# Another order of steps in an attention-and-ReGLU kernel

## The chip, the core and the metric

The kernel runs on one core of a Trainium2 chip. The core has a matmul engine (TensorE, in the profile PE, its weight loads PEld), a vector engine (VectorE, DVE), an engine for activations (ScalarE, ACT), a general one (GpSimd, POOL) and SyncE (SP), which here only issues transfers. Each takes its instructions in the order in which the program has them. The metric is the device time of one launch in microseconds.

## The reference

```python
B, N, m, C = (4, 12416, 32, 128)
def mab(q, kv):
    s = scale * (q @ kv.transpose(0, 2, 1))
    s = s - s.max(-1, keepdims=True)
    a = np.exp(s)
    a /= a.sum(-1, keepdims=True) + 1e-09
    return a @ kv
h = mab(I, x)
attn = mab(x, h)
...
gate = np.maximum(x @ w_gate, 0.0)
val = x @ w_val
out = gate * val @ w_out
```

For each of four batches, 32 inducing vectors attend to the 12,416 rows of x and give h (32 x 128). Then every row attends to those 32 vectors; the result goes through a feed-forward layer with 1,536 hidden units, where "x" is the attention's result.

## The kernel before

A row's attention output is a weighted mean of 32 vectors. The sign of a gate is settled for each hidden unit and batch; with it the layer's output is a quadratic form in the 32 softmax weights. The kernel works on that form: products of two weights are exponentials of sums of two scores, and a table T per batch (built from h and the three weight matrices) takes 512 such products and 128 single terms to the 128 outputs. Were a sign not certain, a general kernel would run at the end; the flag for this is read near the end by all engines.

A batch has 97 tiles of 128 rows. Four tiles make a block, four blocks a quad "q", six quads and one rest tile a batch. These are the steps, and where their instructions run:

- **E** (`scores`, L558): two matmuls of 32 rows by 512 columns, each on its own row group of PE, make sums of scores in `e_ps` (two buffers); ACT takes the exponential of both into an `F` tile (L576; 20 buffers). 49 per batch.
- **O** (`outputs`, L583): one tile of 128 rows of the result. Four matmuls L591 with F as weights and one L593 with the single terms `p`, 128 rows by 129 columns. After three tiles DVE divides (`rzo` L607, `osb` L608) out of `o_ps` (two buffers); after six, SP stores `osb` (four buffers, L617). 97 per batch.
- **p** (lane of `plan_phase1`, L673): the first attention of the next batch: for batch 1 six turns on PE (L698), then for all `score` (L707, ACT L709), `sums` (L720, L729, DVE L742), `h_end1`, `h_end2` (the DVE chain in `halves`, L130), four `gates` (PE L347, ACT L362, DVE L364), signs and `masked` (L451).
- **u** (products and tables): DVE makes products of gate and value columns (L473, L482), PE sums them with `wo` into the tables (L519, ACT's cast L522; the fifth table L539, DVE L546). T has two buffers, by batch.
- **s**: scores of a quad for the second attention (`pair_out`, L648: PE L372, DVE L628 and L640), and the bounds for the certainty of the signs (L381 to L446, two DVE reductions, one matmul, three POOL instructions).
- **x** (`pair_exp`, L652): ACT's exponential of a quad's scores (L655), which O reads as `p`.
- **l** (`load`): POOL starts the load of one quad of x (`load_x`, L82), cast to 16 bits. Where a turn has been issued since the last load, POOL first reads one value of the turned tile (L681), so that the load starts after it has landed. `x16` has nine buffers.
- **t** (`turn`): SP starts a transposing transfer of the last loaded quad (`turn_x`, L88, the instruction at L91). `xT` has twelve buffers. SP's queue is the one that the stores use.

A first part (`first_batch`, L158) and the first steps of batch 0 stand in a fixed order. From there the string `ORDER` says which step comes next: each letter takes the next step of its lane. Each lane keeps its own order; the string sets how the lanes are interleaved, and with that the order on every engine. The loop at the end of `quadratic_body`:

```python
for step in ORDER:
    if step == "E":
        scores(*next(units))
    elif step == "O":
        b, t = next(tiles)
        g = b * NSLOT + t // TPB
        outputs(b, t)
        if g == B * NSLOT - 3 and t % TPB == 0:
            cond = nc.values_load(flag.left[0:1, 0:1])
    else:
        lanes[step].pop(0)()
```

Below, E71 or O128 is the state after so many E's and O's of the string.

Of the kernel before, what the change touches and what calls it, by code (L numbers as in the profile page):

```python
# [26 lines left out]
def quadratic_body(ctx, tc, x, inducing, moe_w_gate, moe_w_val, moe_w_out, out):  # L27
# [860 lines left out]


ORDER = (  # L890
    "EOpOsExOpOEEpOOOEOOEppOEuEpOOOpEEspOOxOOpOllEElsplOOpOEEOlOOOppEEpOppOpEsEpOpOOEEpOOpEpE"
    "OOOxOsEEOOOpOpEOOpOpOtEpEOpOOEOOpOtEOEtOEuOuOOuxtOOEtusEOuOuEOOOEuuOOxEsuuEuOOOEslsOEOuu"
    "OsuluEEOpOOOEEuOEpEuOpOEEuuuOOxuOOuEEssOOOxOEEpOpuOOOtEuuEupOOtpOEEOuOOOEEOppOOOEEsOOOOl"
    "OlxEEOOpxOOOEEOlOOlOpOEEspxOOOOEEOlOOOpOEEOOOpEOEppOOEEOOpOtpEEpOOpOOOOEEOOtpOOpOEOEOOpO"
    "EsExOOOtutOEEuOOOutOEOuussEOEOOOExuuuOOEElsOOOupluuOEsEsOOEOuxOuEEpuOpEuEuOuOxOOEEOuOOOu"
    "uEOOEsuEuOOEEtuOOpEOuOupOEuEOOtOpEsEOOpuEEsOOOOOEEOOOxOpsEEOOOOpOOEEpOpOOOxOEEspOOpOEOpE"
    "OEppEOOEOOppOEOppOOEpEOOOpOOEOOEpOxOOuOEEuOOOsEOuOOuusEOEOuEOOuEEuuOOOEOOOEsuEOxuOOOEEus"
    "sOOuExuOOOxuEEsuEOuOEOOuEOOEOOOxEuEuOuOOOOEsEuOuOEEOOOOOuEEuuOOOOOEEOuOsEEOOOEOOOxOOOEEO"
    "OOOOOEEOOxOOOOEEOOOOOOEEOOOOOxOEEOOOOOOEEsOOxOOOEEOOOOOsEEOOOOOsEEOOOOsOOEEOOOOOOEEOsOOE"
    "OEOOOxsOOEEOOOOOEsOEOOOxOEEOOOOOOOOOOOO"  # L900
)


# [202 lines left out]
```

## Time and profile before

| | |
|---|---|
| median of 4 runs | 273.33 us (272.33 to 274.58) |
| the profiled execution | 272.81 us |
| its span, first to last instruction | 270.9 us |
| PE, ACT, DVE, POOL busy | 252.2, 228.3, 214.5, 27.3 us |
| start of the first step of the string | about 38.3 us |
| end of the last O's matmuls | 264.4 us |
| transfers | 48.38 MB, mean 179 GB/s |

Busy time is the sum of an engine's instructions; PE's are modelled as to their ends. In a timeline, x4 stands for four instructions of one line that follow each other; the time in brackets is the engine's idle time before the first of them, and what ended it. Loads of one quad land after 10.3 us at the median, turns after 5.0 us, stores after 3.0 us.

### The profile page before, as it was taken

To read this page: it belongs to the slowest core of one execution; us is meant where nothing else is said; L and a number is where in the kernel's file an instruction comes from. 1 tells how busy PE (TensorE), PEld (TensorE's weight loads), DVE (VectorE), ACT (ScalarE), POOL (GpSimd) and SP (SyncE) were. 2 spreads that over 40 slices of the span, in tenths; PEclk is the share of its full clock that TensorE was granted. 3 is DMA by queue.
4 is the path that set the end of the run, shared out by engine and by line. 5 is a ranking of instruction groups with operands and counts; after the bars stand their busy time and mean duration, and the time that the engine had idled before them with its cause. 6 is when DMAs were issued, how large, how long until landed. Compare 5 with 4: busy or idle time off the path is not lost.

```text
span 270.9 us, 9520 instructions
## 1 busy us (share of the span) xinstructions
PE 252.2 (93%) x4029; PEld 188.1 (69%) x4029; DVE 214.5 (79%) x583; ACT 228.3 (84%) x305; POOL 27.3 (10%) x71
## 2 busy tenths in 40 slices
PE   2997799999999999999999999999899999999990
PEld 0795678777676777776667777777677778878770
DVE  4565969757999997775999998778999997688661
ACT  4134699999998999999799999999899989988940
POOL 8372000120000200400003000000010000000000
PEclk9999799999999999999999999999999999999997
DMA  7999986999899989899998979332331234344333
GB/s 184 203 209 204 213 171 79 272 212 246 180 227 189 204 247 210 203 248 261 213 222 214 220 205 186 119 117 85 152 120 60 116 123 154 155 167 161 134 145 110
DMA packets 48738, 48.38 MB, mean 179 GB/s; under 512 B 35472, under 2 KB 36656, under 8 KB 48688
## 3 DMA queue, kind: packets, MB, share of 16 engines
q1 hardware_dynamic: 41520, 33.74, 43.9%
q0 software_dynamic: 6880, 13.50, 27.9%
q8 instruction: 33, 0.54, 0.8%
q10 hardware_dynamic: 288, 0.46, 0.5%
q14 instruction: 17, 0.14, 0.2%
HBM read 27.80 MB, written 25.43 MB: 196 GB/s over the span
## 4 chain that ended last, share of the span: by engine, by line
PE 79%; DVE 8%; ACT 8%; issue 3%; POOL 0%; ACTq 0%; DVEq 0%; POOLq 0%
PE o_ps L591 32%; PE e_ps L569 16%; PE o_ps L593 7%; ACT F L576 5%; PE T_ps L519 3%; PE s_ps L707 3%; PE T_ps L505 3%; PE s_ps L372 3%; DVE osb L608 2%; PE hz_ps L729 2%; PE xT_ps L262 2%; PE T_ps L539 1%; PE s_ps L273 1%; PE hz_ps L720 1%; PE xT_ps L698 1%
## 5 line engine op out<-in xcount | busy, mean ns | idle before, releaser
L576 ACT ACTIVATE F<-e_ps 128x1024 f16<-128x1024 f32 x192 | 185.6, 1026 | 14.6 <-PE e_ps L569 12.1
L591 PE MATMUL o_ps<-T,F 128*128 128x129 f16 x1536 | 129.4, 221 | 1.8 <-DVE osb L608 1.0
L591 PEld LDWEIGHTS <-F 128*128 128x128 f16 x1536 | 98.6, 97 | 27.9 <-issue 19.5
L593 PE MATMUL o_ps<-T,p 128*128 128x129 f16 x388 | 84.5, 218 | 0.0
L608 DVE TENSOR_TENSOR osb<-o_ps,rzo 128x384 f32<-128x384 f32 x132 | 72.5, 549 | 4.8 <-DVE rzo L607 0.2
L569 PE MATMUL e_ps<-sc,sel 32*128 32x512 f16 x384 | 59.6, 382 | 0.5 <-ACT F L576 0.3
L593 PEld LDWEIGHTS <-p 128*128 128x128 f16 x388 | 37.9, 98 | 0.4
L607 DVE RECIPROCAL rzo<-o_ps 128x3 f32<-128x3 f32 x132 | 23.1, 175 | 18.6 <-PE o_ps L593 17.3
L569 PEld LDWEIGHTS <-sel 32*128 32x128 f16 x384 | 16.2, 91 | 18.2 <-issue 5.4
L628 DVE TENSOR_SCALAR sc<-s_ps 128x512 f16<-128x512 f32 (+1 forms) x28 | 17.6, 628 | 2.8 <-PE s_ps L372 2.3
L640 DVE TENSOR_REDUCE reach<-sc 128x1 f32<-128x512 f16 (+1 forms) x28 | 17.6, 627 | 1.0
L655 ACT ACTIVATE p<-sc 128x512 f16<-128x512 f16 (+1 forms) x28 | 16.3, 585 | 0.0
L275 ACT ACTIVATE p<-s_ps 128x256 f16<-128x256 f32 (+3 forms) x16 | 5.3, 332 | 11.5 <-PE s_ps L273 11.5
L263 DVE COPY xT<-xT_ps 128x1024 f16<-128x1024 f16 (+2 forms) x15 | 8.8, 584 | 4.9 <-PE xT_ps L262 3.5
L709 ACT ACTIVATE p<-s_ps 128x512 f16<-128x512 f32 (+1 forms) x21 | 11.4, 548 | 0.7 <-PE s_ps L707 0.7
L442 POOL TENSOR_SCALAR ok<-eps 128x1 f32<-128x1 f32 x4 | 1.2, 289 | 100.6 <-DVE eps L403 100.6
L482 DVE TENSOR_TENSOR U<-U,U 128x1536 f16<-128x1536 f16 (+1 forms) x12 | 10.9, 906 | 0.4
L519 PE MATMUL T_ps<-wo,U 128*128 128x128 f16 x144 | 10.1, 219 | 0.0
L707 PE MATMUL s_ps<-indT,xT 128*128 128x32 f16 x288 | 10.0, 177 | 0.0
L86 POOL DMA_DIRECT2D x<-in_x_dram x18 | 9.7, 552 | 1.7 <-PE xT_ps L262 1.1
L505 PE MATMUL T_ps<-won,U 128*128 128x128 f16 x96 | 7.3, 243 | 2.5 <-ACT won L460 2.5
L372 PE MATMUL s_ps<-xT,h 128*32 128x512 f16 x96 | 9.4, 389 | 0.0
(159 smaller groups left out, 252.2 us busy)
## 6 DMA issues: line engine op xcount, KB each, us to landing
out_dram<-osb SPq DMA_DIRECT2D x64, 384.0 KB, 3.0
x<-in_x_dram POOLq DMA_DIRECT2D x18, 512.0 KB, 10.9
x<-in_x_dram POOLq DMA_DIRECT2D x8, 256.0 KB, 7.7
x<-in_x_dram POOLq DMA_DIRECT2D x5, 128.0 KB, 8.1
osb<-in_x_dram ACTq DMA_DIRECT2D x1, 384.0 KB, 4.4
osb<-in_x_dram SPq DMA_DIRECT2D x1, 384.0 KB, 4.3
wg<-in_moe_w_gate_dram POOLq DMA_DIRECT2D x1, 384.0 KB, 8.0
wv<-in_moe_w_val_dram POOLq DMA_DIRECT2D x1, 384.0 KB, 9.8
```

Of the source, the lines that this page charges most:

```text
L372: nc.tensor.matmul(ps[32 * r : 32 * r + 32, 0:w], state[b]["h2"], xTs(state[b]["xT"], (4 * q + r) * TPB, w // P), start=True, stop=True,)
L519: nc.tensor.matmul(ps, u_cols(0, t, j), wo[:, t, :], start=t == 0, stop=t == NFF - 1)
L569: nc.tensor.matmul(ps[:, r, :], sel4[rows, j, :], sc[rows, :], start=True, stop=True)
L576: act.activation(out=F[b, q, d, j], in_=ps, func=AF.Exp, scale=sm_scale2)
L591: nc.tensor.matmul(ps, f, T[b % 2][:, j, 0 : P + 1], start=j == 0, stop=False)
L593: nc.tensor.matmul(ps, p2s[b, q][rows, tok], T[b % 2][rows, 4 + r, 0 : P + 1], start=False, stop=True)
L607: dve.reciprocal(out=rz[:, 0:k, :], in_=outputs.ps[:, 0:k, P : P + 1])
L608: dve.tensor_tensor(out=osb[:, a6 : a6 + k, :], in0=outputs.ps[:, 0:k, 0:P], in1=rz[:, 0:k, :].broadcast_to([P, k, P]), op=ALU.mult,)
L628: dve.tensor_scalar(out=scs[b, q][0:k, 0:w], in0=ps[0:k, 0:w], scalar1=64.0, scalar2=-64.0, op0=ALU.min, op1=ALU.max,)
L640: dve.tensor_reduce(out=state[b]["reach"][0:k, q : q + 1], in_=scs[b, q][0:k, 0:w], axis=AX.X, op=ALU.max, apply_absolute_value=True,)
L655: act.activation(out=p2s[b, q][0:k, 0:w], in_=scs[b, q][0:k, 0:w], func=AF.Exp, scale=sm_scale2)
L707: nc.tensor.matmul(ps[:, t, :], s["xT"][q][:, t, :], indT, start=True, stop=True)
```

## The change

The string `ORDER` is replaced by another with the same number of each letter (831 in all). No other line is touched.

```diff
 ORDER = (
-    "EOpOsExOpOEEpOOOEOOEppOEuEpOOOpEEspOOxOOpOllEElsplOOpOEEOlOOOppEEpOppOpEsEpOpOOEEpOOpEpE"
-    "OOOxOsEEOOOpOpEOOpOpOtEpEOpOOEOOpOtEOEtOEuOuOOuxtOOEtusEOuOuEOOOEuuOOxEsuuEuOOOEslsOEOuu"
-    "OsuluEEOpOOOEEuOEpEuOpOEEuuuOOxuOOuEEssOOOxOEEpOpuOOOtEuuEupOOtpOEEOuOOOEEOppOOOEEsOOOOl"
-    "OlxEEOOpxOOOEEOlOOlOpOEEspxOOOOEEOlOOOpOEEOOOpEOEppOOEEOOpOtpEEpOOpOOOOEEOOtpOOpOEOEOOpO"
-    "EsExOOOtutOEEuOOOutOEOuussEOEOOOExuuuOOEElsOOOupluuOEsEsOOEOuxOuEEpuOpEuEuOuOxOOEEOuOOOu"
-    "uEOOEsuEuOOEEtuOOpEOuOupOEuEOOtOpEsEOOpuEEsOOOOOEEOOOxOpsEEOOOOpOOEEpOpOOOxOEEspOOpOEOpE"
-    "OEppEOOEOOppOEOppOOEpEOOOpOOEOOEpOxOOuOEEuOOOsEOuOOuusEOEOuEOOuEEuuOOOEOOOEsuEOxuOOOEEus"
-    "sOOuExuOOOxuEEsuEOuOEOOuEOOEOOOxEuEuOuOOOOEsEuOuOEEOOOOOuEEuuOOOOOEEOuOsEEOOOEOOOxOOOEEO"
-    "OOOOOEEOOxOOOOEEOOOOOOEEOOOOOxOEEOOOOOOEEsOOxOOOEEOOOOOsEEOOOOOsEEOOOOsOOEEOOOOOOEEOsOOE"
-    "OEOOOxsOOEEOOOOOEsOEOOOxOEEOOOOOOOOOOOO"
+    "pEsEOOOOOxEEpOpOEpEOEOsEpOOxEEOOOppOEEsplOOpOxEEpsOOlpOOEEuOOlOpOOpEEppOOEppOOEEpsllOlpO"
+    "EEpOEppOlOEOOEpOpOOEEsOOpOOEsOOOpEEspOpOOEOEOOpEtOOxuOOEEOuOOOttuEtOsutEuOuOEOtEOsEOuOxO"
+    "uEuuEOOOpOutuEEOOEpsEOuupEuEOuuupEOxpEOxuuOOOpsEEOuOOpuuOEuEpOOupOxOEEslpOuOOpOEEllpOupO"
+    "EEOpOxOOlOEEpOOOpEOOEOOEsEOOOpOEEOtOpOpOOOtEEOOpOOOEEOOtpOOOEpOtEpOOOOsuxEEOpuOOOOEuEpul"
+    "lOOlpOEEsOuOOOEpuEOOxOuusEuEpuOOuOOOEEusOOOuEEptxuOusOOOOEEsuEOOEsOEEtOuOOEOOOpxOEtEsxpO"
+    "OOOuOEEOOuuOOpOEEspOOOuEEOOpuEEOuOuuOpuEOpOOEEpupxEEOOpOOEpOOpOOEEOOOOpOsEEOOOOpOEpEOOO"
+    "OpEOOEpOOOxOEEOOOuuOEOOEusEOOEOuOEOOEuxOOuOOEEuOOuuOEEuOOOuxOOOuEEOOOususEEOOxOOOOEEsOO"
+    "OuEssuxEEOOOOEuxOOEEuOOuOEOOuOsEEOOOuuEuEOOOOuEOOEOEuOOEOuxOOsEEOOOOuEEsOOOOEEOOOOOEEOOO"
+    "OOOxEEOOOOEOOEOOOOxEEOOOOOEsEOOOOEEsOOEOOOEOOOOEEOOOOOsEEOOxOOOOEEOOOOOOEEOsxOOOOsEEOsOO"
+    "OOEEOOOOOsxEEOOOOOOEEOOOOEOOEOOOOOOOOOO"
 )
```

For example the seven turns of batch 2 stood at E25, 28, 30, 31, 32, 51 and 53 and stand at E34, 36, 36, 37, 37, 39 and 43; its loads 4 and 5 stood after five of the turns and stand before all of them; and batch 3's `h_end1` stood at E121 and stands at E109.

More of the change, by code (lines that the diff above doesn't have):

```diff
@@ L890 @@
 ORDER = (
-    "EOpOsExOpOEEpOOOEOOEppOEuEpOOOpEEspOOxOOpOllEElsplOOpOEEOlOOOppEEpOppOpEsEpOpOOEEpOOpEpE"
-    "OOOxOsEEOOOpOpEOOpOpOtEpEOpOOEOOpOtEOEtOEuOuOOuxtOOEtusEOuOuEOOOEuuOOxEsuuEuOOOEslsOEOuu"
-    "OsuluEEOpOOOEEuOEpEuOpOEEuuuOOxuOOuEEssOOOxOEEpOpuOOOtEuuEupOOtpOEEOuOOOEEOppOOOEEsOOOOl"
-    "OlxEEOOpxOOOEEOlOOlOpOEEspxOOOOEEOlOOOpOEEOOOpEOEppOOEEOOpOtpEEpOOpOOOOEEOOtpOOpOEOEOOpO"
-    "EsExOOOtutOEEuOOOutOEOuussEOEOOOExuuuOOEElsOOOupluuOEsEsOOEOuxOuEEpuOpEuEuOuOxOOEEOuOOOu"
-    "uEOOEsuEuOOEEtuOOpEOuOupOEuEOOtOpEsEOOpuEEsOOOOOEEOOOxOpsEEOOOOpOOEEpOpOOOxOEEspOOpOEOpE"
-    "OEppEOOEOOppOEOppOOEpEOOOpOOEOOEpOxOOuOEEuOOOsEOuOOuusEOEOuEOOuEEuuOOOEOOOEsuEOxuOOOEEus"
-    "sOOuExuOOOxuEEsuEOuOEOOuEOOEOOOxEuEuOuOOOOEsEuOuOEEOOOOOuEEuuOOOOOEEOuOsEEOOOEOOOxOOOEEO"
-    "OOOOOEEOOxOOOOEEOOOOOOEEOOOOOxOEEOOOOOOEEsOOxOOOEEOOOOOsEEOOOOOsEEOOOOsOOEEOOOOOOEEOsOOE"
-    "OEOOOxsOOEEOOOOOEsOEOOOxOEEOOOOOOOOOOOO"
+    "pEsEOOOOOxEEpOpOEpEOEOsEpOOxEEOOOppOEEsplOOpOxEEpsOOlpOOEEuOOlOpOOpEEppOOEppOOEEpsllOlpO"
[3 more added lines that the diff above has]
+    "lOOlpOEEsOuOOOEpuEOOxOuusEuEpuOOuOOOEEusOOOuEEptxuOusOOOOEEsuEOOEsOEEtOuOOEOOOpxOEtEsxpO"
+    "OOOuOEEOOuuOOpOEEspOOOuEEOOpuEEOuOuuOpuEOpOOEEOpupxEEOOpOOEpOOpOOEEOOOOpOsEEOOOOpOEpEOOO"
+    "OpEOOEpOOOxOEEOOOuuOEOOEusEOOEOuOEOOEuxOOuOOEEOuOOuuOEEuOOOuxOOOuEEOOOususEEOOxOOOOEEsOO"
+    "OuEssuxEEOOOOEuxOOEEuOOuOEOOuOsEEOOOuuEuEOOOOuEOOEOEuOOEOuxOOsEEOOOOuEEsOOOOEEOOOOOEEOOO"
+    "OOOxEEOOOOEOOEOOOOxEEOOOOOEsEOOOOEEsOOEOOOEOOOOEEOOOOOsEEOOxOOOOEEOOOOOOEEOsxOOOOsEEOsOO"
+    "OOEEOOOOOsxEEOOOOOOEEOOOOEOOEOOOOOOOOOO"
 )
```

## The prediction

> **What bounds the kernel now.** I read four views, in this order: busy times on the page, busy time by stage, the timeline of one engine at a time, and the waits.
>
> The page:
>
> ```profile
> PE 252.2 (93%) x4029; PEld 188.1 (69%) x4029; DVE 214.5 (79%) x583; ACT 228.3 (84%) x305; POOL 27.3 (10%) x71
> L576 ACT ACTIVATE F<-e_ps 128x1024 f16<-128x1024 f32 x192 | 185.6, 1026 | 14.6 <-PE e_ps L569 12.1
> L591 PE MATMUL o_ps<-T,F 128*128 128x129 f16 x1536 | 129.4, 221 | 1.8 <-DVE osb L608 1.0
> ```
>
> TensorE leads. A busy PE need not be at its peak, so I look at starts. The timeline of some steps (start, duration, instruction):
>
> ```profile
> 217.16 0.40 PE L591 MATMUL o_ps<-T,F 128*128 128x129 f16 x4
> 217.45 0.40 PE L591 MATMUL o_ps<-T,F 128*128 128x129 f16 x4
> 217.74 0.40 PE L591 MATMUL o_ps<-T,F 128*128 128x129 f16 x4
> 218.03 0.40 PE L591 MATMUL o_ps<-T,F 128*128 128x129 f16 x4
> 218.27 0.22 PE L593 MATMUL o_ps<-T,p 128*128 128x129 f16 x1
> 218.42 0.78 PE L569 MATMUL e_ps<-sc,sel 32*128 32x512 f16 x4
> ```
>
> One output step "O" (four L591 matmuls, one L593) follows the last after 0.29 us, five matmuls at 58 ns, without a gap. An O that is followed by a score step "E" takes 0.39 (218.03 to 218.42), so 0.10 more. A single E before an O takes 0.32 (251.82 to 252.14 in the timeline); two E's 0.54 (216.32 to 216.86), so the first 0.22 and the switch again 0.10. **TensorE's work can therefore be added up step by step.** From 38.3, where the written order takes over: 388 O at 0.29 = 112.5; 191 E at 0.227 = 43.4; 309 switches of shape (counted below) at 0.095 = 29.4; the rest (tables 0.68 each, scores of the next batches 0.40, sums 0.42, pair scores 0.23, gates 0.15, PE turns 0.46) about 39.3. Sum 224.6, so the last O would end at 262.9. In the trace it starts at 263.85 and ends at 264.4. TensorE is late by 1.5 us in all. The busy view by stage says 3.4 (226.10 less 222.70):
>
> ```profile
> 38.30:264.40 226.10, 222.70 (x3513) 165.06 (x3511) 189.30 (x508) 209.80 (x264) 11.80 (x30) 1.00 0.69 177
> 122.30:140.30 18.00, 16.64 (x221) 11.82 (x220) 14.86 (x43) 16.36 (x21) 0.00 (x0) 1.00 0.95 237
> 182.30:200.30 18.00, 17.17 (x234) 12.44 (x232) 16.43 (x48) 16.66 (x22) 0.00 (x0) 1.00 0.29 112
> 254.30:260.30 6.00, 5.77 (x84) 4.49 (x82) 3.97 (x16) 5.33 (x8) 0.21 (x1) 1.00 0.35 135
> ```
>
> Columns: stretch, length, then PE, PEld, DVE, ACT, POOL busy, clock, DMA share. PE's idle time is 1.36 + 0.83 in two stretches; these are where the next batch's h is finished and its gates are made. At the end 0.23 and 0.50 more; before 122.3 only 0.36 (83.64 of 84 busy), elsewhere 0.12. In the first of the two stretches the chain is visible:
>
> ```profile
> 126.16 0.46 DVE L364 TENSOR_SCALAR gb<-hw_ps 128x282 f16<-128x282 f32 x1 [0.96 <-ACT ga L362]
> 126.67 0.31 PE L347 MATMUL hw_ps<-hT,wv 128*128 128x48 f16 x6 [0.40 <-DVE gb L364]
> 130.15 0.41 PE L591 MATMUL o_ps<-T,F 128*128 128x129 f16 x4 [0.64 <-DVE osb L608]
> ```
>
> DVE waits in order for gates that ACT has not emptied, the o_ps evictions stand behind it, and PE waits for an o_ps bank. **Only such idle time can be won**: the work itself is not changed.
>
> **What the Trainium skill says.** TensorEngine Tiling (Array Packing), Key Properties: changing the tiling mode drains TensorE. This trace agrees: about 0.095 us at each change between the 128-row O and the 32-row E. TensorE: Matmul & The Clock Gate, "Wait — 56ns, not 53.3ns?": N / 2.4 GHz plus 2.5 ns, an estimate of 56.3 ns for 129 columns; here 58. Perfetto Trace Analysis, Per-engine timelines: the end of a matmul is modelled; so I count starts. DMA: Bandwidth & Descriptors, "Issuing engines are not separate DMA queues": loads, turns and stores share the same 16 DMA engines; here their share stays at 0.95 up to 122 us and falls to 0.3 after 170.
>
> **The change part by part.** All counts of steps are the same (388 O, 191 E, 82 u, 75 p, 40 s, 27 x, 14 l, 14 t), and each lane keeps its own order. Nothing is removed or added but two POOL casts: L681 runs twice after the first time instead of three times, at 0.2 us on an idle POOL: nothing.
>
> (a) *Switches of shape.* I walk both strings with three shapes: full (O, tables, gates, transposes, s1, the ones-sums), row tiles (E), column tiles (pair scores, hz, table5). Before 309 changes, after 306: 3 x 0.095 = **-0.3 us**, on the path.
>
> (b) *The chain of the next batch is spread.* From hend1 to masked, batch 2 took 8 E and 19 O (E71-79, O128-147), now 12 E and 28 O (E63-75, O102-130); batch 3 7 E and 15 O (E121-128), now 11 E and 24 O (E109-120). Gates: 6 E for batch 2 (E73-79), now 8; 5 for batch 3, now 8. The products and tables of batch 2 took E81-105 and now E75-106, of batch 3 E128-156, now E122-153. The same waits of DVE for ACT (0.96 and 0.94 us for batch 2's gb and vb) get more PE work between their ends, and DVE's load, 5.83 of 6 us in the stages that begin at 134 and 152, is thinner. These two stretches hold 2.19 us of PE idle. The gain lies between 0 and 2.19; I take half, **-1.1 us**.
>
> (c) *Batch 1* goes the other way a little: masked at E33/O54 instead of E28/O49, and table3 at O96 instead of O93, with O98 as its first reader. By the sum, its 12 matmuls end 1.4 us before O98 starts; ACT's cast (0.27) stands behind at most one running F (1.03). Batches 2 and 3 already ran with such margins (table3 end to first reader about 0.9 and 1.2 us) and show no wait there. Bounds 0 to +0.5; I take 0.
>
> (d) *The loads.* Batch 2's seven come before all its turns, so only the first waits for a landed turn (53.3 us); the last two were issued at 89.1 and 90.4. They landed 3.5 us apart (59.9, 63.6, 66.5, 70.2): two more land at about 74 and 77. POOL has nothing else to do. Batch 3's last three go together behind the turn at E74.
>
> (e) *Turns on SP's queue.* Batch 2's stand at E34, 36, 36, 37, 37, 39, 43 instead of E25, 28, 30, 31, 32, 51, 53: the first at about 78 us, after the last load's 77. Their readers (score0 88.7, score1 92.5, score2 95.6) come after 78 + 3.2 per turn + 5.0 to landing. No engine waited for a turn before; I take 0, and its bad end is the rival below. Batch 3's turns lie further apart (E69, 69, 73, 74, 89, 95, 97 with a store between nearly all), with 5 us and more before their readers.
>
> (f) *The end.* After the last E come 10 O instead of 12, but PE's work is the same; the last F's wait (0.19, at 260.78) may go, inside what I took. The register load of the flag still stops PE 9 O before the end (0.49 at 261.57).
>
> Sum: -0.3 - 1.1 = **-1.4 us** on the profiled execution's own 272.81 (span 270.9 and 1.9 around it): 271.4. The median of the runs is 273.33, 0.5 above it, so 271.9.
>
> **The rivals.**
>
> 1. *The idle time only moves.* Another order of three engines that are 79 to 93% busy brings waits of its own: for it speaks that ACT is over 90% busy in most stages and DVE in many, against it that the chains got longer room. -0.3 and 0 to 0.8 back: about 273.3.
>
> 2. *Slower: SP's queue holds the stores.* Four turns now stand between the stores of O54-59 and O60-65. Before, SP was held thus:
>
> ```profile
> 71.15 3.95 SPq L91 DMA_TRANSPOSE xT<-x  x1
> 75.20 0.53 SPq L617 DMA_DIRECT2D out_dram<-osb  x1
> 75.83 4.54 SPq L91 DMA_TRANSPOSE xT<-x  x2
> 80.46 1.25 SPq L617 DMA_DIRECT2D out_dram<-osb  x1
> 81.81 4.23 SPq L91 DMA_TRANSPOSE xT<-x  x1
> ```
>
> That is 3.2 us a turn: four from 82.2 end at 95, the store lands 3.0 later at 98. Its osb buffer (four exist) is wanted again by the eviction after O86, at about 100.5. Margin 2.5 us, so it decides from 3.8 us a turn. At 5.0 us (the median to landing, as if turns did not overlap) the store lands at 105: DVE stands 4.7 us, PE's two o_ps banks cover about 1.7, so +3.0: 276.3.
>
> 3. *All idle goes*, in both stretches and at the end: -0.3 - 2.2 - 0.4 = -2.9: 270.4. Against it: E and O still compete with DVE in every stage.
>
> **How the numbers follow.** The forecast (-0.5 to -2.2) has 0.47; rival 1 0.28; rival 3 or a little beyond 0.15; rival 2 0.10. A change under 1% (2.7 us) cannot be told from none here. Rival 3 reaches that bound only with all it has or a median that falls well, so faster 0.19; slower is rival 2 for the most part, 0.08; within 1% 0.73. The range takes in rival 3, rival 1 and half of rival 2's cost, with the scatter of the medians (272.3 to 274.6 in four runs): 270.1 to 274.3.
>
> **What would show it.** PE idle in the two batch changes (now about 10 us earlier) falls to 1.1 or less; the sum of busy PE stays at 252. PE waits for osb evictions around 100 us, or an SP turn over 3.8 us, would show rival 2. A fall of more than 3 us would say that my step costs contain waits, and then the prediction is wrong in its first part.

## The result, and the profile after

| | median | ratio to the kernel before, 95% interval |
|---|---|---|
| before | 273.40 us (53 runs) | |
| after | 272.42 us (32 runs) | 0.9966 [0.9949, 0.9983] |
| after, in a later comparison (a_again) | 272.35 us (22 runs) | 0.9968 [0.9949, 0.9987] |

The change is worth 0.9 us: a small gain, seen twice, and below the 1% that the prediction counts as a difference. Runs with a like mean of TensorE's granted clock, without three slow ones of the changed kernel, differ by 1.1 us on average: 272.8 against 273.9 at 0.975 to 0.985, and 271.4 against 272.5 at 0.985 to 0.995. The profiled execution has a span of 270.5 us (270.9 before). The same rows of the page:

```profile
PE 250.8 (93%) x4029; PEld 187.2 (69%) x4029; DVE 214.0 (79%) x583; ACT 228.6 (85%) x305; POOL 26.2 (10%) x70
L576 ACT ACTIVATE F<-e_ps 128x1024 f16<-128x1024 f32 x192 | 185.1, 1025 | 13.4 <-PE e_ps L569 11.0
L591 PE MATMUL o_ps<-T,F 128*128 128x129 f16 x1536 | 128.5, 221 | 2.6 <-DVE osb L608 2.1
```

ACT waits 1.2 us less for its scores (13.4 against 14.6), PE waits 1.1 us more for evictions (2.1 against 1.0). Both can be true at once, and the busy view by stage shows how. The first two rows are the stretch from the string's first step to the last O's matmuls, after and then before; the others are the stages of the kernel after that moved most (stretch, length, then PE, PEld, DVE, ACT, POOL busy, clock, DMA share, GB/s):

```profile
38.96:263.95 224.99, 220.61 (x3515) 163.59 (x3513) 189.09 (x508) 210.02 (x265) 10.77 (x29) 1.00 0.70 177
38.10:264.40 226.30, 222.90 (x3515) 165.06 (x3511) 189.50 (x509) 209.94 (x265) 11.80 (x30) 1.00 0.69 177
112.30:130.30 18.00, 17.69 (x266) 13.32 (x264) 15.13 (x45) 17.19 (x23) 0.00 (x0) 1.00 1.05 218
170.30:188.30 18.00, 17.14 (x242) 12.33 (x241) 15.78 (x40) 16.74 (x22) 0.00 (x0) 1.00 0.29 112
78.30:84.30 6.00, 5.28 (x67) 3.61 (x65) 5.67 (x17) 5.35 (x7) 0.00 (x0) 1.00 0.81 195
248.30:254.30 6.00, 4.90 (x65) 3.58 (x62) 4.45 (x16) 5.04 (x7) 0.61 (x3) 1.00 0.35 139
```

(The string's first E starts at 38.10 before; the prediction's row from 38.30 begins inside it.) PE's busy time fell by 2.3 us and its idle time **rose** from 3.40 to 4.38, so the stretch is 1.3 us shorter. The two profiled executions as wholes differ by only 0.6, because the first part, the same code, took 0.86 us longer after; its half clock (a granted clock of 0.5) lasted 6.8 us instead of 3.4. A second execution of the kernel after (a_again) has the same busy time in the stretch, 220.72, but 5.38 of idle; 1.1 of that is one stop that nothing in the profile explains (last section). So these two traces agree on the busy time to about 0.1 us and on the idle time only to 1 us.

In the two batch changes, taken as stretches of 18 us, the idle time fell from 2.19 to 0.31 + 0.86 = 1.17. But the stretch of before holds batch 2's first four products, and the one of after ends just ahead of them. In the next 4 us PE stands another 0.41:

```profile
130.30:134.30 4.00, 3.59 (x72) 2.49 (x69) 3.90 (x12) 3.59 (x6) 0.18 (x1) 1.00 1.04 328
```

Counted to the same step, the fall is therefore 2.19 to 1.58, that is 0.6 us, and all of it in batch 2 (1.36 to 0.72); batch 3 has 0.86 where it had 0.83. Idle time appeared in two stages that had next to none before, 78.3 to 84.3 and 248.3 to 254.3:

```profile
78.30:84.30 6.00, 5.96 (x75) 4.18 (x72) 5.79 (x17) 5.74 (x9) 0.00 (x0) 1.00 1.07 227
248.30:254.30 6.00, 5.98 (x86) 4.98 (x85) 3.88 (x13) 5.56 (x7) 0.40 (x2) 1.00 0.35 134
```

(These two rows are of the kernel before.) The timeline of PE after names what it waited for in each:

```profile
81.60 0.41 PE L591 MATMUL o_ps<-T,F 128*128 128x129 f16 x4 [0.72 <-DVE osb L608]
...
254.35 0.38 PE L812 MATMUL flag_ps<-v,ones 128*128 128x1 f32 x2 [1.13 <-DVE v L810]
```

and the timeline of DVE what stood ahead of that eviction, and of that v:

```profile
78.97 0.75 DVE L451 TENSOR_TENSOR ga<-ga,on 128x576 f16<-128x576 f16 x1
79.64 0.75 DVE L451 TENSOR_TENSOR gb<-gb,on 128x576 f16<-128x576 f16 x1
80.31 0.55 DVE L473 TENSOR_TENSOR U<-ga,va 128x768 f16<-128x768 f16 x1
80.98 0.56 DVE L608 TENSOR_TENSOR osb<-o_ps,rzo 128x384 f32<-128x384 f32 x1
...
253.26 0.18 DVE L607 RECIPROCAL rzo<-o_ps 128x3 f32<-128x3 f32 x1
253.47 0.56 DVE L608 TENSOR_TENSOR osb<-o_ps,rzo 128x384 f32<-128x384 f32 x1
253.95 0.15 DVE L809 TENSOR_REDUCE v<-kept 128x1 f32<-128x12 f32 x1
254.14 0.16 DVE L810 TENSOR_TENSOR v<-v,near 128x1 f32<-128x1 f32 x1
```

Near 80 us the masking of batch 1 and its first product hold DVE for 1.8 us on end (78.97 to 80.78) while finished tiles fill both o_ps banks. In the kernel before, an eviction stood between them (DVE's timeline), and the flag's matmul, with an E between it and the last O, waited 0.23 us (PE's):

```profile
74.59 0.75 DVE L451 TENSOR_TENSOR gb<-gb,on 128x576 f16<-128x576 f16 x1
75.26 0.17 DVE L607 RECIPROCAL rzo<-o_ps 128x3 f32<-128x3 f32 x1
75.47 0.56 DVE L608 TENSOR_TENSOR osb<-o_ps,rzo 128x384 f32<-128x384 f32 x1
75.95 0.55 DVE L473 TENSOR_TENSOR U<-ga,va 128x768 f16<-128x768 f16 x1
```

```profile
257.01 0.38 PE L812 MATMUL flag_ps<-v,ones 128*128 128x1 f32 x2 [0.23 <-DVE v L810]
```

At 254 us in the kernel after, the flag step stands right behind an O that completes a group of three. DVE takes that eviction first, then makes `v`; PE, with the flag's matmul next in its order, waits for both. Behind the flag PE is late with the next E, so that ACT idles 1.68 us.

Last, SyncE, where the prediction placed its slow rival (its queue from 79 to 96 us):

```profile
79.52 2.88 SPq L91 DMA_TRANSPOSE xT<-x  x1
82.51 0.50 SPq L617 DMA_DIRECT2D out_dram<-osb  x1
83.12 12.66 SPq L91 DMA_TRANSPOSE xT<-x  x4
95.87 0.54 SPq L617 DMA_DIRECT2D out_dram<-osb  x1
```

Four turns take 12.66 us, 3.17 each, and the store goes out at 95.9. Only POOL waits for turns, ahead of its loads, as the kernel intends and as it did before; DVE never waits for a store.

### The profile page after: what moved, and what is told of

Same layout as the page of the kernel before. It is cut to its first block, busy times and chain, and to the rows that moved or that the text cites. A ratio compares the mean times of both kernels' runs of the same rounds, so it can differ in the third digit from the quotient of the medians.

```text
span 270.5 us, 9525 instructions
## 1 busy us (share of the span) xinstructions
PE 250.8 (93%) x4029; PEld 187.2 (69%) x4029; DVE 214.0 (79%) x583; ACT 228.6 (85%) x305; POOL 26.2 (10%) x70
## 4 chain that ended last, share of the span: by engine, by line
PE 73%; DVE 12%; ACT 8%; issue 4%; POOL 0%; ACTq 0%; DVEq 0%; POOLq 0%
PE o_ps L591 29%; PE e_ps L569 15%; ACT F L576 6%; PE o_ps L593 6%; DVE osb L608 4%; PE T_ps L505 3%; PE T_ps L519 3%; PE s_ps L707 3%; PE s_ps L372 2%; PE xT_ps L262 2%; PE hz_ps L729 2%; DVE U L473 1%; PE s_ps L273 1%; PE xT_ps L698 1%; PE hz_ps L720 1%
## 5 line engine op out<-in xcount | busy, mean ns | idle before, releaser
L576 ACT ACTIVATE F<-e_ps 128x1024 f16<-128x1024 f32 x192 | 185.1, 1025 | 13.4 <-PE e_ps L569 11.0
L569 PE MATMUL e_ps<-sc,sel 32*128 32x512 f16 x384 | 59.5, 385 | 0.3
L569 PEld LDWEIGHTS <-sel 32*128 32x128 f16 x384 | 15.2, 91 | 18.3 <-issue 6.4
L505 PE MATMUL T_ps<-won,U 128*128 128x128 f16 x96 | 8.1, 259 | 2.5 <-DVE U L473 2.5
L505 PEld LDWEIGHTS <-U 128*128 128x128 f16 x96 | 7.3, 120 | 4.2 <-DVE U L473 4.1
```

The lines of the kernel that those rows point to most:

```text
L505: nc.tensor.matmul(s["T_ps"][j // 2][:, j % 2, :], u_cols(i, t, j), won[:, t, :], start=False, stop=(i, t, j % 2) == (1, NFF - 1, 1),)
L569: nc.tensor.matmul(ps[:, r, :], sel4[rows, j, :], sc[rows, :], start=True, stop=True)
L576: act.activation(out=F[b, q, d, j], in_=ps, func=AF.Exp, scale=sm_scale2)
```

## The experiments

All ran beside the kernel before on the same chip (273.09 us in the first four, 273.38 in the next four, 273.49 in the last four). Where two versions are compared that didn't run together, their ratios to before are.

### Do neighbouring E steps run at the same time?

What the sum of the prediction left out: two E steps in a row cost 0.54 us when both read the same rows of `sc`, and can cost 0.32 when their units lie on disjoint row groups; then all four matmuls start together. In the trace after, both kinds stand close to each other:

```profile
199.68 0.39 PE L569 MATMUL e_ps<-sc,sel 32*128 32x512 f16 x4
...
205.67 0.60 PE L569 MATMUL e_ps<-sc,sel 32*128 32x512 f16 x4
```

The duration column is enough: four matmuls in 0.39, the duration of a pair, or in 0.60. Of the places where one E directly follows another, the strings have 29 on disjoint rows ("disjoint neighbours") before and 34 after; by their starts I count 20 and 23 concurrent ones. Four kernels permute the units of E under an unchanged string:

```diff
-    units = iter(units[5:])
+    units = units[5:]
+    units = iter([units[i + k] for i, k in enumerate(SHIFT)])
```

**a_min**: the order after, 2 of its 66 neighbours disjoint.

> The string of the changed kernel, with the E steps' units taken in a slightly other sequence, so that of the 66 places where an E directly follows an E on TensorE only 2 have the two E's on different row groups (34 in the changed kernel). Theory 'pairs' (two neighbouring E's on disjoint row groups run at the same time, which saves 0.21 us each; 23 of 34 did so in the trace of the changed kernel): about 21 x 0.21 = 4.4 us slower than the changed kernel, 3.5 us slower than the one before. Theory 'waits' (the gain came from the chain of the next batch that got more room): as the changed kernel, 0.9 us faster than before, within 1 us.

279.71 us, 1.0229 [1.0185, 1.0273]. One pair ran concurrently. The page has E at 64.8 us busy instead of 59.5, and a wait of E for its scores that the permutation itself brought in:

```profile
L569 PE MATMUL e_ps<-sc,sel 32*128 32x512 f16 x384 | 64.8, 386 | 3.5 <-DVE sc L628 2.7 <-issue 0.5 <-ACT F L576 0.3
```

Of some 7 us lost against after, where the expectation had 4.4, 22 pairs at 0.21 come to 4.6 and that wait to 2.7. So concurrency is real and on the path.

**a_max**: 60 of 66 disjoint.

> The same string, units in a sequence that puts 60 of the 66 neighbouring E's on disjoint row groups. 'Pairs': if two thirds of the 26 added ones run at once, 17 x 0.21 = 3.6 us faster than the changed kernel, less what ACT then holds back (it is busy 210 of 225 us in this stretch), so 1.5 to 3.6 us; against before 2.4 to 4.5 us faster. 'Waits': no change from the changed kernel, 0.9 us faster than before.

271.95 us, 0.9962 [0.9939, 0.9984]: no different from after, though 35 pairs ran concurrently and E's busy time fell to 55.9. PE waits instead: 1.0 us for F, 0.5 for scores, 2.5 for evictions (after: 0.3 for the first two together, 2.1 for evictions). Beyond what after has, this source gives nothing that shows; that ACT and DVE do not go faster is the likely reason.

**a_29** (after, with as many disjoint neighbours as before) and **b_34** (before, with as many as after).

> The string of the changed kernel with 29 disjoint neighbours, as many as before had. 'Pairs': the part of the gain that they brought is lost, 3 to 5 pairs x 0.21 = 0.6 to 1.0 us slower than the changed kernel, 0 to 0.3 us faster than before. 'Waits': as the changed kernel, 0.9 us faster than before.

> The string of before, units so that 34 neighbours are disjoint, as in the changed kernel. 'Pairs': 0.6 to 1.0 us faster than before, so as the changed kernel within 0.4 us. 'Waits': no change from before.

a_29: 273.73 us, 1.0023 [1.0002, 1.0043], that is 1.6 us above after. Five pairs at 0.21 would be 1.05, but the trace has only one concurrent pair fewer (22), and 1.1 us in one wait of E for `sc` that the permutation brought. It is inconclusive. b_34: 273.03 us, 1.0002 [0.9982, 1.0021]: three pairs more, as many as after has, and no gain. So the three pairs that the change made concurrent (0.6 us of PE's work) aren't shown to be its gain.

### Room in the chain of the next batch

**a_tight**: the order after, with `h_end1` to the last gate of batches 2 and 3 pressed together: both parts of `h_end` in a row, and the four gates within a few O's.

```diff
-    "EEOpOxOOlOEEpOOOpEOOEOOEsEOOOpOEEOtOpOpOOOtEEOOpOOOEEOOtpOOOEpOtEpOOOOsuxEEOpuOOOOEuEpul"
+    "EEOpOxOOlOEEOOOEOOEOOEsEppOOOOpEEOptOpOOpOOtEEOOOOOEEOOtpOOOEpOtEpOOOOsuxEEOpuOOOOEuEpul"
...
-    "OOOuOEEOOuuOOpOEEspOOOuEEOOpuEEOuOuuOpuEOpOOEEOpupxEEOOpOOEpOOpOOEEOOOOpOsEEOOOOpOEpEOOO"
+    "OOOuOEEOOuuOOpOEEspOOOuEEOOpuEEOuOuuOpuEOpOOEEOpuxEEOOOOEOOOOEEppOOOOppOsEEOOppOOOOEpEOOO"
```

> The changed kernel with the chain from h_end1 to masked of batches 2 and 3 pressed into as little room as before: batch 2 from E67 instead of E63 to E75 (8 E and 21 O, as 8 E and 19 O before), batch 3 from E114 instead of E109 to E120 (6 E and 16 O, before 7 and 15); nothing else moves. Theory 'room' (the prediction's largest term): the 1.1 us are lost, so 0.2 us slower than before, and TensorE stands idle there again. Rival 'elsewhere' (the idle time in these stretches only moved, the gain came from E's that run at once and from fewer changes of shape): as the changed kernel within 0.4 us, 0.9 us faster than before.

277.56 us, 1.0144 [1.01, 1.0187]: 4.8 us more than after, and 3.9 more than before, where the theory of the room had 0.2. Its busy view for the two batch changes, and PE's timeline in them:

```profile
115.30:133.30 18.00, 16.43 (x208) 12.28 (x205) 13.11 (x40) 13.95 (x18) 0.00 (x0) 0.91 0.87 212
172.30:190.30 18.00, 15.13 (x220) 11.51 (x216) 12.81 (x39) 14.24 (x20) 0.00 (x0) 1.00 0.29 111
```

```profile
120.19 0.41 PE L756 MATMUL h_ps<-zs,ones 128*128 128x32 f32 x2 [1.00 <-DVE zs L746]
125.68 0.31 PE L347 MATMUL hw_ps<-hT,wv 128*128 128x48 f16 x6 [0.43 <-DVE gb L364]
```

Idle time of 1.57 + 2.87 = 4.44 us stands where after has 1.17. Between DVE's, ACT's and PE's turns in this chain there is too little other work. But this is twice the 2.19 that before had with as little room, so the room alone doesn't set the cost: a_tight shows that pressing this chain costs time, and not how much of it the change gained. The rest of the loss isn't settled. The profiled execution has half clock after the stop (0.91 in the first row; last section), but two runs at a mean clock of 0.997 still took 275.8 and 275.9 us, against 270.6 to 271.9 for the runs of after at 0.993 or more.

### The flag, and the block on DVE

**a_flag**: the flag step two O's and two E's later, after O368.

```diff
-    "OOEEOOOOOsxEEOOOOOOEEOOOOEOOEOOOOOOOOOO"
+    "OOEEOOOOOxEEOOsOOOOEEOOOOEOOEOOOOOOOOOO"
```

> The changed kernel with the step of the flag two O and two E later (after O368, not right behind O366). In the trace of the changed kernel TensorE stood 1.13 us before the flag's matmul, because DVE first divides O364 to O366, and ACT then stood 1.68 us. If TensorE's wait is on the path: 0.8 to 1.1 us faster than the changed kernel, 1.7 to 2.0 faster than before. If the end has cover: no change from the changed kernel.

271.02 us in nine runs, 0.992 [0.9888, 0.9951], 1.3 us below after by the ratios, with intervals that just touch. The stage that had 1.10 us of idle has 0.02, and the one near 80 us is as in after:

```profile
78.30:84.30 6.00, 5.28 (x66) 3.45 (x62) 5.67 (x16) 5.36 (x7) 0.46 (x1) 1.00 0.92 226
...
248.30:254.30 6.00, 5.98 (x83) 4.62 (x80) 4.10 (x18) 5.70 (x8) 0.62 (x3) 1.00 0.34 134
```

**a_flag2**: as a_flag, and batch 1's first two products one and two tiles later.

```diff
-    "EEpOEppOlOEOOEpOpOOEEsOOpOOEsOOOpEEspOpOOEOEOOpEtOOxuOOEEOuOOOttuEtOsutEuOuOEOtEOsEOuOxO"
+    "EEpOEppOlOEOOEpOpOOEEsOOpOOEsOOOpEEspOpOOEOEOOpEtOOxOOuEEOOuOOttuEtOsutEuOuOEOtEOsEOuOxO"
```

> The changed order with two things more: the flag step after O368 instead of O366, as in a_flag, and the first two products of batch 1 one and two tiles later (after O58 and O60), so that VectorE does not run the two masking operations of 0.75 us and a product of 0.55 us back to back while four finished tiles wait for their normalisation. Theory that idle removed is time gained: the stop of TensorE of 0.72 us near 80 us goes, and the time is 0.7 us below that of a_flag, ratio about 0.989. Rival, that the stop only moves (the products then collide with the tiles that follow, and the table of batch 1 comes later): as a_flag, 0.992, with an idle stretch of equal size at 81 to 90 us.

270.61 us in six runs, 0.989 [0.985, 0.9929]. PE has 5.75 us busy of the six near 80 us, where after has 5.28, and no new stop up to 92 (8.00 busy of the next 8). **It beats both kernels**: its interval lies below that of after in the same comparison. That the second step adds to a_flag is likely by the trace, but the two intervals overlap.

**a_best**: a_flag2 with 60 of 66 neighbours disjoint, and **a_again**: after itself beside it.

> As a_flag2, and the units of the F tiles put in the order that makes 60 of the 66 neighbouring E steps lie on disjoint rows. Theory that the gain of concurrent E steps is used up by ScalarE and the tiles' own waits as it was in a_max: the same as a_flag2 within 0.5 us, ratio 0.988 to 0.993. Rival, that it was eaten by the two stops that a_flag2 removes: 2 us or more below a_flag2, ratio 0.982.

> The changed kernel itself, once more, on the chip of the other three, so that each of them has the changed kernel beside it as well as the one before. Ratio to the kernel before: 0.9966 if the first comparison holds (0.995 to 0.998). If it comes out at 1.000 or above, the gain of 0.9 us lies within what differs from chip to chip and no step of the prediction can be called right by the total.

a_best: 270.89 us, 0.9931 [0.9909, 0.9954], no better than a_flag2. PE's busy time falls to 218.07 of 223.91 us in the string's stretch, that is 5.84 us idle: faster matmuls turned into waiting, with the flag's stop gone and the one near 80 us down to 0.2 us. a_again: 0.9968, as in the table above.

### Turns and stores on SyncE's queue

**a_turns**: the order after, with batch 2's turns and its loads 4 and 5 where they stood before (three lines of the string).

> The changed kernel with batch 2's turns, and its loads 4 and 5, at the places they had before (E25, 28, 30, 31, 32, 51, 53; loads E38, E39): SP no longer issues four turns on end. The prediction costed this at nothing: as the changed kernel within 0.4 us. If the turns on SP's queue held the stores or the stores' landing, it would be faster than the changed kernel by what they held, up to 3 us; if the new places of loads and turns brought the gain, as before.

273.41 us, 0.9978 [0.9957, 0.9999]: within the error of after. Where the turns stand is worth nothing that shows, either way.

**a_osb3**: after with three output tiles, and **b_osb3**: before with three (the first part, which borrows these tiles, is changed alike).

```diff
-            osbs[0] = mt([P, 6, P], FP32, "osb", 4)
+            osbs[0] = mt([P, 6, P], FP32, "osb", 3)
```

> The changed kernel with three osb buffers instead of four. SP issued the store of O60 to O65 at 95.9, it lands at about 99; with four buffers its buffer is wanted after O86 at about 100.5, with three after O80 at about 96. If the four turns are near to deciding, as the slower rival had it: DVE stands about 3 us there, 2 to 3 us slower than the changed kernel. If stores have much more room than that: no change.

> The kernel before, with three output tiles (osb) instead of four. Theory that the four turns standing together on SyncE's queue made the changed order depend on the fourth tile: with the order of before, whose turns stand apart, three tiles cost little, ratio below 1.005. Rival, that what needs the fourth tile is any store that lands late (9.4 us from issue to landing in both kernels while the loads of a batch run, at 105.5 us after and 115.5 us before): the same loss as in a_osb3, ratio 1.010 to 1.018, with VectorE held for 2 to 4 us by a store issued near 115 us.

a_osb3: 277.29 us, 1.014 [1.0092, 1.0189]. b_osb3: 274.85 us, 1.0039 [1.0018, 1.006]. That only the changed order loses much suits the theory of the stacked turns; the place doesn't. In a_osb3 DVE waits 6.1 us in three places: 1.1 and 1.6 us that end at 55.5 and 78.0, before batch 2's first turn (79.7), and the longest here (DVE's timeline, and the store it waited for in the chain of waits):

```profile
115.60 0.56 DVE L608 TENSOR_TENSOR osb<-o_ps,rzo 128x384 f32<-128x384 f32 x1 [3.38 <-DMA out_dram<-osb]
```

```profile
105.68 9.83 DMA out_dram<-osb
```

The four turns had left the queue at 94; this store was issued without delay and took 9.8 us to land, while the next batch's loads were on. With four tiles such a store takes as long: the one issued at 105.5 us in the trace after, and the one at 115.5 before, took 9.4. b_osb3 has the same wait behind a store of 9.0 us, with DVE held 2.0 us. So the fourth tile covers slow landings among loads, not turns ahead of a store. Why after suffers more from three tiles than before (6.1 us of waits against 2.5) isn't settled.

## Why the prediction was right, and where not

The forecast, 271.9 us, is 0.5 from the median of 272.42, and its -1.4 is close to the -1.3 by which the string's stretch got shorter. That is in good part luck: the terms are wrong in both directions, and the errors met.

**The step that failed is "only such idle time can be won: the work itself is not changed".** TensorE's idle time, 3.40 us, rose by 1.0; its busy time, which the prediction held fixed, fell by 2.3. The sum of steps (224.6) hid this. It agreed with the trace to 1.5 us, but it priced 20 concurrent pairs of E steps at 0.54; with 0.21 off for each the steps come to 220.4, so that TensorE was late by 5.7 us, of which the profile shows 3.4 as idle. The rest must be waits inside busy time. An estimate from the starts points the same way: O steps that took over 0.06 us longer than the quickest tenth of those before the same kind of step add up to an excess of 3.6 us before and 2.0 after. That step costs might contain waits the prediction did consider, but only for a fall of more than 3 us.

**(a) was too small.** It took -0.3 for three switches of shape. PE's busy time fell by 2.3 instead. Counted from each step's start to the next, less idle time, O steps take 125.4 us of the stretch instead of 126.8, the largest part, and E steps 50.7 instead of 50.9. For the O's most of it are the hidden waits just named (an O followed by another starts 0.29 us before it in both traces, at the median). The prediction read "two E's 0.54" off one pair and priced all pairs with it, though some in the same trace took 0.32; three more of these account for 0.6 at most. Which step of the new order removed which hidden wait, no run here separates.

**(b) had the right sign and about half its size.** Forecast -1.1 by halving 2.19 us of idle. Counted to the same step it fell by 0.6, to 1.58, and only in batch 2; batch 3's chain, which got longer room as well, gained nothing. a_tight supports the cause, since without the room 3.3 us of idle return, but not the size.

**(c) failed.** It bounded batch 1 at 0 to +0.5, took 0, and looked at table 3. What cost 0.7 us was `masked`, which the new order puts next to the first product, so that DVE is held for 1.8 us. The step looked for a late reader and not for what queues behind the moved instructions on their own engine.

**(d) and (e) held.** Loads and turns cost nothing that shows. ("No engine waited for a turn" leaves out POOL, which waits for them by design.) Four turns went out in 12.66 us against 4 x 3.2, the store at 95.9 against "95". It landed after 4.6 us rather than 3.0, at 100.5; but the eviction that wants its buffer came at 103.0, later than the 100.3 of the old order, so that the margin was 2.5 us all the same. Rival 2 named the right buffer and the wrong cause of a late store.

**(f) failed.** The end was put at 0 because "PE's work is the same". The flag step had moved from behind an E to right behind a full group of three tiles. That cost 0.9 us of PE idle between 248.3 and 260.3 (0.25 before, 1.15 after), and a_flag, which moves one letter, gains 1.3 us.

In all: busy time -2.3, batch changes -0.6, block at 80 us +0.7, flag +0.9, elsewhere 0. This is -1.3. **Rival 1**, that idle only moves, was thus true of the idle time as a whole, which even grew. What kept the result on the forecast's side was the fall in busy time; the sign "the sum of busy PE stays at 252" failed (250.8), and the sign for the batch changes, 1.1 or less, was just missed at 1.17 and clearly at 1.58.

## What to carry to other kernels

When an order is changed, list for each moved step what stands directly ahead of it on every engine that it uses, small steps too: one matmul whose operand is made behind an eviction cost as much as the whole change gained. Price a repeated instruction from several places of the trace, since the same two steps can cost 0.54 or 0.32 by the rows that they use. Compare two orders between the same steps, not between the same times, and don't take TensorE's busy time for its work: short waits lie in it. Where three engines are 79% busy or more, shorter steps on one can turn into waiting, as in a_max; what paid here was to remove single stops of the leading engine, as in a_flag.

## What the hardware showed

**Half clock also followed short stops.** The Trainium skill (TensorE: Matmul & The Clock Gate, "Part 1: The HAM clock gate") has free-running windows of 3,413 ns, and its table has half clock after at least one idle one. The windows agree: half clock comes in pieces of 3.4 or 6.8 us here. But none of the windows before such a piece in mid-run was idle as a whole; in three cases PE had stopped for about a third to a half of it. a_turns (PE's timeline, then its busy view):

```profile
97.34 0.29 PE L591 MATMUL o_ps<-T,F 128*128 128x129 f16 x2
98.74 0.29 PE L591 MATMUL o_ps<-T,F 128*128 128x129 f16 x2 [1.11 <-issue]
```

```profile
95.70:99.10 3.40, 2.29 (x49) 1.53 (x42) 3.06 (x6) 3.40 (x6) 0.00 (x0) 1.00 0.90 268
99.10:102.50 3.40, 3.40 (x47) 2.43 (x45) 1.72 (x4) 0.60 (x2) 0.00 (x0) 0.50 0.28 75
```

The same follows 1.0 us of idle in a_tight (121.3 us) and 1.7 in a_osb3 (115.2); a_tight and a_min had it after 0.33 and 0.53 as well. It isn't a rule: stops of 1.44 us in a_tight near 185 us, 1.13 at the flag in after and 1.10 near 64 us in a_again had no such sequel. In the head of the profiled executions the half-clock piece is 3.4 us before, 6.8 after and absent in a_again.

**PE stops within a group of matmuls.** The 1.11 us above fall between the second and third matmul of one O, where nothing that the profile shows is waited for. Such stops stood at 64 to 67 us in a_tight, a_max, a_best, b_34, a_min and a_again (0.3 to 1.1 us), so in the changed kernel itself they come in one execution and not in another. What causes them stays open.
